# Logits of a spectral mixer made ahead of its last stage, and each batch routed in one piece

## The chip, the cores and the metric

The kernel runs on one core of a Trainium2 chip. The metric is the device time of one execution in microseconds; of several executions the median is given. TensorE (PE) multiplies matrices, its weight loads are shown as PEld; VectorE (DVE), ScalarE (ACT) and GpSimd (POOL) do the rest, and SyncE (SP) issues most DMAs.

## The reference

Two blocks follow each other: a global filter by Fourier transform along the tokens, and a mixture of experts of which each token uses the one with the largest logit. All is float32: 8 batches of 2496 tokens with 256 features, 8 experts with 1024 hidden units.

```python
X = np.fft.rfft(x, axis=1)
Y = X * (filt_r + 1j * filt_i)[None, :, :]
y = np.fft.irfft(Y, n=x.shape[1], axis=1).reshape(B * S, D)
logits = y @ w_gate
expert_idx = np.argmax(logits, axis=1)
gate_w = softmax(logits)[np.arange(N), expert_idx]
for e in range(E):
    rows = expert_idx == e
    out[rows] = gate_w[rows, None] * (np.maximum(y[rows] @ w1[e], 0) @ w2[e])
```

## The kernel before

**The transform.** 2496 = 39 x 64, so the transform of a batch is a two-dimensional one over 39 values of q and 64 values of t, in four stages of matmuls. Stage a (L348) transforms over q, three values of t at a time, and stores its result in DRAM (`zd`). Stage b (L362) reads it turned and transforms over t; VectorE multiplies the result by the filter (L369 to L378). Stage c (L388) transforms back over t: for two frequencies f at a time, it leaves in one bank of PSUM 128 rows (real and imaginary parts of 64 values of t) by 2 x 256 features. The bank is evicted and stored as u in DRAM (`ud`). Stage d (L407) reads u with 120 rows, 40 frequency parts for each of three values of t, and its matmul with the table `tds` gives y: 117 tokens (three t, 39 q) in each of 22 columns of a batch. Batch 0 keeps z and u on the chip, transposed, with features on the rows, and turns them by TensorE (`first_a`, `turn_z`, `first_c`, `turn_u`).

**Logits and routing.** After stage d, `turn_y` transposes y by TensorE (L482, 44 transposes a batch), VectorE or ScalarE evicts `yt`, and `logits` (L496) multiplies by the gate matrix `wg`, padded to 32 columns, so that four matmuls for four column strips share a bank `lt`. `turn_logits` (L507) turns the result back to tokens by experts. `route` works on at most 8 columns, so three times a batch: VectorE finds each token's expert (L529 to L543), TensorE counts the tokens of each expert ahead of each token with a triangular matrix and a matrix of ones (L554, L555), VectorE turns the counts into row numbers (L562 to L577). GpSimd then writes a token number and a gate beside each row of y and scatters the rows to DRAM in the order of experts (L615), one DMA for each column. Six tiles of y (`YB`) wait for that.

**Experts.** `tile_map` lists tiles of 128 to 512 rows of one expert. For each tile SP loads its rows (`xg`, `ng`) and the expert's weights (`w1t`, `w2t`), VectorE transposes the rows in blocks of 32x32 (L748), TensorE forms the hidden layer (L791, in a scheme with sums of quarters, or L832) and the result (L849), and GpSimd scatters the rows of the result to the output (L855).

**Order.** The order on TensorE, VectorE, ScalarE and SP is that in which the program emits instructions. Each engine works through its own in that order and waits where an operand isn't there. A planner at build time makes the order: `slot(k)` lists steps of batch k+1 (stage a), k (b and c) and k-1 (d and what follows), each with a place within the slot, the load that it needs and a cost; the main loop keeps a modelled clock `now`, emits the next step or, by a share, a step of the experts, and asks `sides` (routes, tile maps) for a few instructions after each. Stores are emitted one step after they are ordered (`move`, `flush`), loads of the next z, u and x as buffers come free (`more_loads`), weights and rows of tiles by `prefetch`. `evac` gives an eviction to VectorE or ScalarE, whichever the model has free first. PSUM has seven banks for all stages and one, `lt`, for the logits.

Of the kernel before, what the change touches and what calls it, by code (L numbers as in the profile page):

```python
# [19 lines left out]
P = 128  # L20
# [100 lines left out]
def kernel(  # L121
# [44 lines left out]

    perm = ctx.enter_context(tc.tile_pool(name="perm", bufs=1))
# [25 lines left out]
    wg = cst.tile([P, DH, CT], F32, name="wg")  # L193
# [3 lines left out]
    WM = 8  # L197

    seg = cst.tile([P, E, WM + 1], F32, name="seg")
    tot = cst.tile([P, E, WM + 1], F32, name="tot")  # L200
# [7 lines left out]
    tau_i = pro.tile([1, 64], I32, name="tau_i", bufs=1)  # L208
    pools = {}
# [31 lines left out]
    HP = P // 2  # L241
    CH = [(i0, min(4, NG - i0)) for i0 in range(0, NG, 4)]
# [23 lines left out]
    def load_rest():  # L266
        nc.sync.dma_start(out=tds, in_=td)
        nc.vector.memset(wg, 0.0)
        nc.sync.dma_start(out=wg[:, :, :E], in_=moe_w_gate.rearrange("(i p) e -> p i e", p=P))
        nc.sync.dma_start(out=ids0, in_=ids)  # L270
        nc.sync.dma_start(out=vld, in_=valid)

    def make_constants():
# [7 lines left out]
        nc.gpsimd.memset(tot, 0.0)  # L281
        nc.gpsimd.iota(prow, pattern=[[0, 1]], base=0, channel_multiplier=1)
# [18 lines left out]
    ins, outs, lgs, yts, lands = {}, {}, {}, {}, {}  # L301
    NIN, YB = 7, 6
# [78 lines left out]
    def stage_c(b, f):  # L381
# [7 lines left out]
        evac(uo[:, j:j + 2, :], p.rearrange("p (i d) -> p i d", i=2), 512)  # L389
        if j == 2:  # L390
            f0 = f - 2
            move(ud[b][:, f0:f0 + 4, :], uo[:HP])
            move(ud[b][:, NF + f0:NF + f0 + 4, :], uo[HP:])
# [3 lines left out]
    def stage_d(b, c):  # L397
        if c == 0:
            lgs[b] = sb.tile([TP, NG, E], F32, tag="lg", name="lg")
# [76 lines left out]
    def turn_y(b, c):  # L476
        yo = outs["o", b, c]
        for j in range(0, CH[c][1], 2):
            pt = bank().rearrange("p (i q) -> p i q", i=4)
            for i in range(2):  # L480
                for dh in range(DH):
                    nc.tensor.transpose(  # L482
                        pt[:, 2 * i + dh, :TP], yo[:, j + i, dh * P:(dh + 1) * P], ident[:TP, :TP]
                    )
            yt = yts[b, c, j] = sb.tile([P, 4, TP], F32, tag="yt", name="yt", bufs=4)
            evac(yt, pt[:, :, :TP], 4 * TP)

    def logits(b, g):

        js = range(min(4, NG // 2 - 4 * g))  # L490
        w = len(js) * CT
        pair = [yts.pop((b, 2 * g + j // 2, 2 * (j % 2))).rearrange("p (i h) q -> p i h q", i=2) for j in js]
        lt = psr.tile([P, 2, E * NG], F32, tag="lt", name="lt")[:, :, :TP]
        for dh in range(DH):
            for j in js:
                mm(lt[j * CT:(j + 1) * CT], lhsT=wg[:, dh, :], rhs=pair[j][:, :, dh, :],  # L496
                   start=(dh == 0), stop=(dh == DH - 1))
        ls = sb.tile([P, 2, TP], F32, tag="ls", name="ls", bufs=1)
        evac(ls[:w], lt[:w], 2 * TP)
        outs["l", b] = (g, w, ls)  # L500

    def turn_logits(b):
        g, w, ls = outs.pop(("l", b))
        n = w // CT
        pt = bank()[:TP, :2 * w].rearrange("p (i w) -> p i w", i=2)
        for i in range(2):
            nc.tensor.transpose(pt[:, i, :], ls[:w, i, :], ident[:w, :w])  # L507
        evac(lgs[b][:, 8 * g:8 * g + 2 * n, :].rearrange("p (j i) e -> p i j e", i=2),
             pt.rearrange("p i (j c) -> p i j c", c=CT)[:, :, :, :E], 16 * n)

    scatters, rows_at, held_y = {}, {}, [0]


    def route(b, c0, c1):

        t0 = 4 * c0
        w = min(4 * c1, NG) - t0
        lg = lgs[b][:, t0:t0 + w]
# [3 lines left out]
        def small(name, *shape, dt=F32, tag=None):  # L522
            n = int(np.prod(shape))
            full = sb.tile([TP, WM * n // w], dt, tag=tag or name, name=name, bufs=1)[:, :n]
            return full.rearrange("p (a b) -> p a b", a=shape[0]) if len(shape) == 2 else full

        yos = [outs.pop(("o", b, c)) for c in range(c0, c1)]
# [5 lines left out]
        yield 2  # L533
        nc.vector.tensor_tensor(ex, lg, mx[:, :, None].to_broadcast(sh3), op=ALU.subtract)
        nc.vector.tensor_tensor(oh, oh, em8[:TP, None, :].to_broadcast(sh3), op=ALU.mult)
        yield 2
        idx = small("idx", w)
        nc.vector.tensor_reduce(idx, oh, axis=AX.X, op=ALU.min)
        if t0 + w == NG:

            nc.vector.tensor_tensor(idx, idx, vld[:, t0:t0 + w], op=ALU.mult)
# [4 lines left out]
        yield 3  # L546
# [13 lines left out]
        free["s"] = max(free["s"], now[0]) + 1.2  # L560
        sd = small("sd", w)
# [3 lines left out]
        yield 3  # L565
# [4 lines left out]
        yield 2  # L570
        nc.vector.tensor_tensor(pos, pos, oe, op=ALU.mult)
        row = sb.tile([TP, WM], U32, tag="row", name="row", bufs=2)[:, :w]
        rowf = small("rowf", w)
        nc.vector.tensor_reduce(rowf, pos.rearrange("p e t -> p t e"), axis=AX.X, op=ALU.add)
        yield 2
        nc.vector.tensor_copy(row, rowf)
        nc.vector.tensor_copy(cnt, tot[:, :, w])  # L577
        yield 2
        for i, yo in enumerate(yos):
            n = min(4, w - 4 * i)  # L580
            sh8 = (TP, n, 8)
            nc.gpsimd.tensor_scalar(
                yo.bitcast(I32)[:, :n, D:D + 8], in0=ids0[:, t0 + 4 * i:t0 + 4 * i + n, None].to_broadcast(sh8),
                scalar1=float(b * S), scalar2=None, op0=ALU.add,
            )
            nc.gpsimd.tensor_copy(yo[:, :n, D + 8:], sd[:, 4 * i:4 * i + n, None].to_broadcast(sh8))
# [569 lines left out]
```

## Time and profile before

| what | value |
|---|---|
| median of 6 executions | 1564.94 us (1553.47 to 1566.86) |
| the profiled execution, its own time | 1565.88 us |
| its span, first to last instruction | 1564.2 us |
| mean granted TensorE clock | 0.980 |
| DMA packets, megabytes, mean rate | 215173, 276.82 MB, 177 GB/s |
| share of 16 DMA engines of SP's queue | 54.1% |
| SP waiting to reload `w1t` (L742) for TensorE (L791) | 232.1 us, 54 times, longest 11.7 |
| SP waiting to reload `w2t` (L738) for TensorE (L849) | 101.3 us, 30 times, longest 9.5 |

The busy time of an engine is the time in which it works on at least one instruction; matmuls overlap, so the time of a sequence is read from the starts of its members rather than from the duration of one. A granted clock of 0.5 means that TensorE runs at half speed. "Idle before" a group is the time in which the engine had nothing to do before an instruction of that group, with the engine, the tile and the line that ended it.

### The profile page before, as it was taken

Reading aid. Unit: us, or ns where it says so; the run is one execution under the profiler, and the core shown is the slowest. Engines: PE = TensorE matmul, PEld = TensorE weight load, DVE = VectorE, ACT = ScalarE, POOL = GpSimd, SP = SyncE. Lnnn points to the kernel's source line nnn. Section 1 sums busy time; section 2 is a strip of 40 time slices with the busy share of each in tenths; the row PEclk is TensorE's granted clock in tenths of the full one; section 3 lists DMA queues with packets and bytes.
Section 4 is the critical chain, followed back from the end, with each engine's and each line's share of the span. In section 5 each row is a group of like instructions: output and inputs, shape, how many; then the busy total and the mean of one; then the engine's idle time right before and its main releaser. Section 6 shows DMA issues by size and latency. Waiting matters only on the chain. (4 is left out here: it accounts for less than half of the span.)

```text
span 1564.2 us, 23882 instructions
## 1 busy us (share of the span) xinstructions
PE 1487.0 (95%) x7202; PEld 1169.3 (75%) x7202; DVE 751.7 (48%) x1676; ACT 478.7 (31%) x993; POOL 696.3 (45%) x910
## 2 busy tenths in 40 slices
PE   7988897899999999999999999999999999999998
PEld 6543454776667876787777876778888889999997
DVE  4677375415664556555674545447343534440000
ACT  3444342233232233222332223222222222223433
POOL 3343244423624555345635545665455546741111
PEclk9999899999999999999999999999999999999999
DMA  9759898887597548835494455455656443455661
GB/s 235 198 162 306 240 274 231 247 209 240 169 248 182 161 144 229 213 109 166 124 231 113 126 145 150 118 151 151 177 155 197 142 142 114 119 186 168 173 193 40
DMA packets 215173, 276.82 MB, mean 177 GB/s; under 512 B 124227, under 2 KB 162508, under 8 KB 215045
## 3 DMA queue, kind: packets, MB, share of 16 engines
q1 hardware_dynamic: 195925, 231.94, 54.1%
q0 software_dynamic: 19120, 43.33, 8.1%
q8 instruction: 61, 1.00, 0.3%
q14 instruction: 67, 0.55, 0.1%
HBM read 195.19 MB, written 80.64 MB: 176 GB/s over the span
## 5 line engine op out<-in xcount | busy, mean ns | idle before, releaser
L795 DVE TENSOR_TENSOR hT<-bank,hT 128x512 f32<-128x512 f32 (+1 forms) x504 | 300.4, 628 | 327.3 <-PE bank L791 203.6
L849 PE MATMUL bank<-w2t,hT 128*128 128x256 f32 x1984 | 446.7, 383 | 5.2 <-ACT hT L799 3.5
L849 PEld LDWEIGHTS bank<-w2t,hT 128*128 128x128 f32 x1984 | 379.0, 192 | 72.8 <-issue 15.7
L855 POOL DMA_INDIRECT out_dram<-ys,ng x161 | 161.6, 1004 | 471.3 <-DMA out_dram<-ys,ng 113.9
L799 ACT ACTIVATE hT<-hT 128x1024 f32<-128x1024 f32 (+1 forms) x144 | 132.4, 956 | 328.7 <-DVE hT L795 315.5
L615 POOL DMA_INDIRECT rows<-yo,row x176 | 177.3, 1008 | 74.9 <-issue 54.5
L791 PE MATMUL bank<-xT,w1t 128*128 128x256 f32 (+1 forms) x864 | 193.9, 361 | 1.5 <-DVE yw L371 0.9
L854 ACT ACTIVATE ys<-bank,ng 128x256 f32<-128x256 f32 x137 | 64.8, 473 | 405.4 <-PE bank L849 308.9
L791 PEld LDWEIGHTS bank<-xT,w1t 128*128 128x128 f32 x864 | 152.9, 192 | 27.4 <-issue 6.8
L791 PE MATMUL bank<-sums,wsum 128*128 128x256 f32 (+1 forms) x576 | 137.1, 361 | 0.5 <-DVE hT L795 0.4
L849 PE MATMUL bank<-w2s,hT 128*128 x592 | 132.6, 379 | 0.0
L832 PE MATMUL bank<-xT,w1t 128*128 128x128 f32 (+1 forms) x864 | 125.9, 301 | 1.8 <-DVE xT L748 1.8
L748 DVE STREAM_TRANSPOSE xT<-xg 128x512 f32<-128x512 f32 (+2 forms) x126 | 57.5, 495 | 145.7 <-PE bank L832 99.7
L832 PEld LDWEIGHTS bank<-xT,w1t 128*128 128x128 f32 x864 | 115.1, 193 | 13.0 <-issue 7.5
L849 PEld LDWEIGHTS bank<-w2s,hT 128*128 128x128 f32 x592 | 110.3, 190 | 13.8
L791 PEld LDWEIGHTS bank<-sums,wsum 128*128 128x128 f32 x576 | 101.7, 192 | 22.0 <-issue 9.4
L369 DVE TENSOR_TENSOR ys<-bank,ht 128x512 f32<-128x512 f32 x80 | 54.9, 687 | 78.2 <-PE bank L362 68.0
L348 PE MATMUL bank<-fin,tas 117*120 117x512 f32 x154 | 77.6, 624 | 6.3 <-DMA fin<-in_x_dram 5.5
L388 PE MATMUL bank<-ys,tcs 128*128 128x512 f32 x140 | 74.0, 612 | 9.9 <-DVE ys L378 6.7
L766 POOL TENSOR_TENSOR wsum<-w1t 128x256 f32<-128x256 f32 x72 | 52.7, 732 | 65.1 <-PE bank L791 63.3
L838 ACT ACTIVATE hT<-bank 128x128 f32<-128x128 f32 (+1 forms) x206 | 61.2, 298 | 51.3 <-PE bank L832 37.6
L362 PE MATMUL bank<-fin,tbs 128*128 128x512 f32 x140 | 72.0, 602 | 2.6 <-DMA fin<-zd 2.0
(143 smaller groups left out, 1626.0 us busy)
## 6 DMA issues: line engine op xcount, KB each, us to landing
w1t<-in_moe_w_dram SPq DMA_DIRECT2D x126, 512.0 KB
w2t<-in_moe_w_dram SPq DMA_DIRECT2D x68, 512.0 KB
fin<-in_x_dram SPq DMA_DIRECT2D x39, 512.0 KB
fin<-zd SPq DMA_DIRECT2D x70, 256.0 KB
ud<-uo SPq DMA_DIRECT2D x70, 256.0 KB
zd<-zo SPq DMA_DIRECT2D x35, 480.0 KB
fin<-ud SPq DMA_DIRECT2D x35, 480.0 KB
xg<-rows SPq DMA_DIRECT2D x112, 128.0 KB
```

Source lines behind the costliest of these rows:

```text
L348: mm(p[:TK, :], lhsT=tas, rhs=xt[:TP, j:j + 2, :], start=True, stop=True)
L362: mm(p, lhsT=tbs, rhs=zi[:, j:j + 2, :], start=True, stop=True)
L388: mm(p, lhsT=tcs, rhs=ys, start=True, stop=True)
L615: sc = nc.gpsimd.indirect_dma_start(out=rowsd, out_offset=bass.IndirectOffsetOnAxis(ap=at, axis=0), in_=what, in_offset=None,)
L791: mm(q[:, v], lhsT=left[:, v * P:(v + 1) * P], rhs=right, start=True, stop=True)
L795: nc.vector.tensor_tensor(o, q, a, op=ALU.add)
L799: nc.scalar.activation(o.rearrange("p v r c -> p v (r c)"), q.rearrange("p v r c -> p v (r c)"), AF.Relu)
L832: mm(p[:, :m], lhsT=w1t[2 * i + g][:, dh, fh, v * P:(v + 1) * P], rhs=xts[i][:, dh, :m], start=(dh == 0), stop=(dh == DH - 1))
L838: lambda: nc.scalar.activation(hT, p[:, :m], AF.Relu))
L849: mm(p[:, :D], lhsT=hs[i][k % 4 // 2][:, k // 4, k % 2, j * P:(j + 1) * P], rhs=w2, start=(k == 0), stop=(k == FT - 1))
L854: lambda: nc.scalar.activation(ys, p[:, :D], AF.Copy, scale=gate))
L855: nc.gpsimd.indirect_dma_start(out=out, out_offset=bass.IndirectOffsetOnAxis(ap=gis[i].bitcast(U32)[:, j, :1], axis=0), in_=ys, in_offset= ...
```

## The change

The logits are linear in y, and y is linear in u over the frequency parts: y = tds^T u for each feature. The changed kernel multiplies u by the gate matrix first and applies `tds` to the eight resulting columns.

For batches 1 to 7, VectorE transposes each bank of stage c in blocks of 32x32 into a tile `tu` of 12 or 8 frequencies, beside the eviction. `u_logits` multiplies these blocks by a gate matrix `wb` that is laid out so that the four blocks of 32 rows (two halves of t, real and imaginary part) get column groups of their own, in 64 matmuls for a batch. One matmul turns each half's result (`turn_logits`), four DMAs for each half store it in DRAM (`vd`, in elements of 32 bytes), and six DMAs load it as `spec`, 120 frequency parts by 22 columns by 8 experts (`load_logits`, emitted five modelled microseconds later). For batch 0 the transposed u is on the chip and is multiplied directly. `logits` is then one matmul with `tds` for a whole batch, and `route` runs once a batch over 22 columns, ahead of stage d. `send_rows` writes numbers and gates and scatters the rows of four columns as soon as stage d has made them; `YB` falls from 6 to 4. `turn_y` and its tiles go.

```diff
@@ stage_c
+        f0, n = HALVES[f >= HALVES[0][1]]
+        if f == f0:
+            outs["t", b] = sb.tile([P, HALVES[0][1], D], F32, tag="tu", name="tu", bufs=1)
+        nc.vector.transpose(outs["t", b][:, f - f0:f - f0 + 2, :].rearrange("p i d -> p (i d)"), p)
+        free["v"] = max(free["v"], now[0]) + 0.7
...
-    def turn_y(b, c):
...
+    def u_logits(b, half=0):
...
+        n = HALVES[half][1] // 4
+        lt = psr.tile([P, HALVES[0][1] // 4, CT], F32, tag="lt", name="lt")[:, :n]
+        tu = outs.pop(("t", b))[:, :4 * n].rearrange("p (g k) d -> p g k d", g=4)
+        for j in range(NJ):
+            for g in range(4):
+                mm(lt[g * CT:(g + 1) * CT], lhsT=wb[:, j, :], rhs=tu[:, g, :, j * CT:(j + 1) * CT],
+                   start=(j == 0), stop=(j == NJ - 1))
+        ls = outs["l", b] = sb.tile([P, HALVES[0][1] // 4 * CT], F32, tag="ls", name="ls", bufs=1)[:, :n * CT]
+        evac(ls, lt.rearrange("p k r -> p (k r)"), n * CT)
...
+    def turn_logits(b, half=0):
...
+        nc.tensor.transpose(pt, ls, ident)
+        evac(vt, pt, P)
+        for m in range(4):
+            move(vd[b][m, f0:f0 + n].rearrange("(g k) r e -> (k r) g e", g=4),
+                 vt.rearrange("p (g m e) -> p m g e", g=4, m=4)[:, m])
+        if half:
+            delayed.append((now[0] + 5.0, lambda: load_logits(b)))
+
+    def load_logits(b):
+        for th in range(2):
+            of = vd[b][2 * th:2 * th + 2].rearrange("c f r e -> (c f) r e")
+            for j in range(NB):
+                i0 = -((j - th * HT) // NB) if th else 0
+                t0 = NB * i0 + j - th * HT
+                n = (HT - 1 - t0) // NB + 1
+                nc.sync.dma_start(
+                    out=spec[b % 2][j * NS:(j + 1) * NS, i0:i0 + n],
+                    in_=of[:, t0:t0 + NB * (n - 1) + 1:NB, :],
+                )
+        lands["v", b] = now[0] + 7.0
+
+    def logits(b):
+        lgs[b] = sb.tile([TP, NG, E], F32, tag="lg", name="lg", bufs=1)
+        p = bank()[:TP, :NG * E]
+        mm(p, lhsT=tds, rhs=spec[b % 2].rearrange("p i e -> p (i e)"), start=True, stop=True)
+        evac(lgs[b].rearrange("p i e -> p (i e)"), p, NG * E)
+        sides.append(route(b))
...
+    def send_rows(b, c):
+
+        while b not in routed:
+            yield "wait"
+        row, sd, at = routed[b]
...
@@ slot
+            for half, (f0, n) in enumerate(HALVES):
+                at = (f0 + n + 4) / (NF + 4) + 0.005
+                steps.append((at, lambda half=half: u_logits(k, half), None, 2.6 if half == 0 else 2.1, "b"))
+                steps.append((at + 0.04, lambda half=half: turn_logits(k, half), None, 0.2, "b"))
...
+                    steps.append((at - 0.04, lambda: logits(k - 1), ("v", k - 1), 0.3, "d"))
...
-                if c >= 3 and c % 2:
-                    steps.append((at + 0.01, lambda c=c: logits(k - 1, (c - 3) // 2), None, 0.9, "d"))
-                if 1 <= c <= nch:
-                    steps.append((at + 0.03, lambda c=c: turn_y(k - 1, c - 1), None, 0.22 * CH[c - 1][1], "d"))
-                if c >= 3 and c % 2:
-                    later = at + (0.07 if k == 1 else 0.11)
-                    steps.append((later, lambda c=c: turn_logits(k - 1), None, 0.25, "d"))
-                    steps.append((later + 0.001, lambda c=c: sides.append(route(k - 1, c - 3, min(c - 1, nch))), None, 0.0, "d"))
+                    steps.append((at + 0.02, lambda c=c: sides.append(send_rows(k - 1, c)), None, 0.0, "d"))
```

## The prediction

> **What bounds the kernel now.** First the page's busy shares and its 40 slices:
>
> ```profile
> PE 1487.0 (95%) x7202; PEld 1169.3 (75%) x7202; DVE 751.7 (48%) x1676; ACT 478.7 (31%) x993; POOL 696.3 (45%) x910
> ...
> PE   7988897899999999999999999999999999999998
> ...
> DVE  4677375415664556555674545447343534440000
> ```
>
> TensorE sets the end: 77 us of the 1564.2 us span are idle. VectorE comes near to binding only in the third and fourth slice, 100 to 140 us. Next the groups of TensorE by shape, for the steps that the change touches (count, busy us, mean ns of one, then idle time before them):
>
> ```profile
> L482 PE MATMUL bank<-ident,yo 117*128 117x117 f32 x352 | 44.8, 269 | 2.2 <-DVE yo L234 2.2
> L496 PE MATMUL lt<-yt,wg 128*32 128x234 f32 x352 | 30.2, 379 | 9.7 <-ACT yt L234 6.7 <-DVE yt L234 2.6 <-issue 0.2
> L507 PE MATMUL bank<-ident,ls 128*117 128x128 f32 x32 | 6.2, 276 | 0.0
> L507 PE MATMUL bank<-ident,ls 96*117 96x96 f32 x16 | 3.2, 283 | 0.5 <-ACT ls L234 0.5
> L554 PE MATMUL bank<-oe,tri 117*117 117x64 f32 x32 | 5.8, 266 | 4.3 <-DVE oe L543 4.3
> L554 PE MATMUL bank<-oe,tri 117*117 117x48 f32 x16 | 3.3, 293 | 9.7 <-DVE oe L543 9.6
> ```
>
> TensorE stood idle 26.4 us before these: 9.7 before the logits (L496), 14.0 before the routing sums (L554). The duration of one is its latency; the price of one in a row is read from starts in the timeline, here at full clock (start, us, count last):
>
> ```profile
> 226.47 1.01 PE L496 MATMUL lt<-yt,wg 128*32 128x234 f32 x16
> 227.41 1.02 PE L482 MATMUL bank<-ident,yo 117*128 117x117 f32 x8
> 228.27 1.03 PE L362 MATMUL bank<-fin,tbs 128*128 128x512 f32 x2
> ```
>
> Sixteen logits instructions take 227.41 - 226.47 = 0.94 us, so four, one for each strip of 32 columns, run side by side in 0.235 us; eight transposes take 0.86 us, 0.107 each. Last the windows of 20 us (PE, PEld, DVE, ACT and POOL busy, granted clock, DMA share, GB/s):
>
> ```profile
> 100.00:120.00 20.00, 15.01 (x45) 5.89 (x44) 16.83 (x36) 6.58 (x17) 8.60 (x11) 0.90 0.69 200
> 120.00:140.00 20.00, 16.68 (x39) 7.03 (x38) 14.93 (x30) 6.21 (x14) 1.97 (x2) 0.93 0.87 287
> ...
> 180.00:200.00 20.00, 15.67 (x53) 8.20 (x53) 9.26 (x25) 6.02 (x17) 5.01 (x9) 0.83 0.81 217
> ...
> 400.00:420.00 20.00, 17.50 (x71) 12.03 (x70) 12.79 (x30) 4.07 (x10) 9.99 (x16) 0.83 0.30 87
> ...
> 1100.00:1120.00 20.00, 20.00 (x94) 17.61 (x93) 10.81 (x17) 5.54 (x7) 10.90 (x16) 1.00 0.58 174
> ```
>
> A gap costs twice: after one of some 2 us the clock is halved for a while. The 3.8 us gap before L496 at 187 us stands in a window granted 0.83, the 2.3 us gap before L554 at 410 us in another. Nine windows with a gap of L482, L496 or L554 above 2 us (at 180, 400, 420, 440, 580, 900, 940, 1000 and 1020 us) were granted 0.83, 0.83, 0.92, 0.91, 0.93, 0.91, 0.91, 0.92 and 0.94: together 0.90 of a window is lacking, 18 us. After 1040 us there is expert work alone, unbroken, and nothing of this change.
>
> **TensorE work.** Removed: 352 transposes of y x 0.107 = 37.7; 88 rounds of logits x 0.235 = 20.7; 48 turns of logits (L507) x 0.11 = 5.3; 24 routing pairs x 0.48 (two passes of L554 and two of L555, 237.41 to 237.89 us in the same timeline) = 11.5. Together 75.2 us. Added, by the instruction order of the changed kernel: 448 small matmuls of 96 or 64 columns, each in two passes, four strips at once, 224 rounds. No row has such a round. From below, 234-column rounds scaled by columns give 112 x 0.096 + 112 x 0.064 = 18; from above, 224 x 0.235 = 53. I take 0.11 us, the start-to-start of a 64-column pass that has to load its weights (L555): 24.6. Eight one-matmul logits (176 columns, two passes, between L555's 0.11 and a 256-column pass's 0.215; by columns 0.148): 2.4. Eight routing pairs of 176 columns: 32 x 0.148 = 4.7. Fourteen turns x 0.11 = 1.5. Batch 0 from the transposed u: four rounds at 0.43 (a 512-column pass), four at 0.235, four passes and six turns at 0.11: 3.7. Together 36.9. **Net -38**, with bounds -45 and -10. Around 100 to 140 us TensorE waits for VectorE anyway, so one batch's share, 38/8 = 5, is not realised: **-33**.
>
> **VectorE.** 70 transposes of a 128x512 bank are added. L748 takes 686 ns from SBUF, a copy of a bank of that size 684 to 690 ns: 0.69 each, 48 us. The 28 evictions of yt and ls (17.2 us) go. Sixteen small operations of a route cost 93 us over 24 routes; eight wide ones, at some 0.37 us each (0.25 us for 64 elements, plus 112 more at the slope 0.69/512 to 0.42/256 = 1.05 ns), cost 8 x 16 x 0.37 = 47. Net -15: nothing is added in busy time. Where TensorE waits for these transposes is priced below.
>
> **Waits removed.** 26.4 us of gaps and 18 us of clock: **-44**.
>
> **Waits added.** (1) The way through DRAM. After the second turn of a batch, eviction 0.4 us, four stores at 0.4 us of SP issue and 2.9 us to the last packet (as the 64-byte loads of ng, 2 to 3 us after issue), six loads at 0.44 and again 2.9: 10.4 us, if SP is free. In the new order TensorE has between that turn and the logits that need it 14.6, 8.6, 15.5, 20.7, 17.3, 15.6 and 7.8 us of work for batches 1 to 7 (counts x starts as above). SP is seldom free: it waited 54 times, 232 us, to reload w1t (4.3 us each) and the stores and loads are queued behind such reloads, behind the gathers of xg and ng, and ahead of the next z, u and weight loads, which come later by as much. With one such wait the way takes 14.7: TensorE idles 6.1 in batch 2 and 6.9 in batch 7, 13 us, and 3 of clock: 16. With none: 4.4. With two (19 us): 34 and some 13 of clock. (2) The routing sums, L554's successors. The seven VectorE steps ahead of them grow from 7 x 0.25 to 7 x 0.37, 0.9 us more. TensorE's cover between logits and sums is 4.3, 4.3, 13.7, 3.4, 4.3, 7.8, 6.9 and 5.2 us; before, by the same count, ten of 24 had under 4.4, and six gaps of 0.4 to 3.3 make up the 14 us. So four gaps of 2 + 0.9 and one of 1: 12.6, and 4 x 2 of clock (18 us over nine gaps): 21; bounds 0 and 8 x 5.3 = 42. (3) Logits that wait for the last VectorE transpose, and turns that wait for the eviction just ahead. In batches 1 to 3 the second half's last three matmuls of stage three are followed at once by the logits: VectorE then has four products (2.8 us) and three transposes (2.1) to do in TensorE's 2.6: 2.3 us each; four turns stand right behind their logits, 0.8 us each; three drops of clock: 15 in all; bounds 0 and 45. A wait of TensorE here holds the expert matmuls behind it; ScalarE and VectorE then run dry, but catch up. **Together +52**, bounds 4 and some 125.
>
> The 98 new DMAs are 0.4 us x 98 = 39 us of SP, whose 377 us of issues leave room, and 5120 packets of 32 bytes a batch. The trace's 64-byte packets take 13.6 ns: 5120 x 13.6 / 16 = 4.4 us of all engines for each batch; the queue's mean packet (54.1% x 16 x 1564 / 195925 = 69 ns) gives 22. Both lie beside other work, except that they lengthen (1).
> The Trainium skill, "DMA: Bandwidth & Descriptors", section "Specifications", speaks against this: it says that a transfer under 512 bytes makes the DMA engine read, modify and write. That would put the 32-byte stores nearer to the 69 ns than to the 13.6 ns, which only 64-byte reads show; the sum above goes by 13.6, and by the other the stores alone would take (69 - 13.6) x 2560 / 16 = 9 us longer for each batch, which would make the forecast the slower rival below. No row here has a 32-byte store to DRAM.
>
> **Sum.** 1565.9 - 33 - 44 + 52 = **1541 us**; its base, the profiled execution, is 0.9 us above the median of 1564.9, so 1540.
>
> **Rivals.**
> A: the new waits are covered. The expert work between the steps speaks for it, the covers of 8 us against it. 1566 - 38 - 44 + 20 = 1504.
> B: the early stretch swallows the gain. VectorE binds until expert work comes in; DMA share is 0.7 to 1.05 up to 400 us. If the work taken off TensorE in three of eight batches only becomes idle time (15) and the waits are 70: 1566 - 23 - 44 + 70 = 1569, no change. For it: gaps before L388 are VectorE's. Against: most routing gaps lie later.
> C, slower: the way through DRAM. If stores sit behind two or three weight reloads and small packets take the mean's time, the way takes 25 us. Then each batch waits at its logits: 10.4, 16.4, 9.5, 4.3, 7.7, 9.4 and 17.2, 75 us, and 7 x 3.4 of clock, 99 in the place of 16: 1624. It decides from a way of some 19.5 us, where (1) reaches 50 and the sum 1575.
>
> **Chances.** Forecast 0.42, A 0.22, B 0.17, C 0.19. The forecast's own range is 1515 to 1565. Faster by over 0.5% (under 1557), which is about what this measurement can tell: most of the forecast and A, 0.62. Within 0.5%: 0.16. Slower: C and a part of B, 0.22. The range for 8 in 10 leaves out the far half of A and of C: 1505 to 1585.
>
> **What would show it.** TensorE's busy time falls by 35 to 40 us; rounds of new logits start some 0.11 us apart; gaps before the one-matmul logits in batches 2 and 7 of 5 to 8 us; gaps of 2 to 3 us before the routing sums; the mean clock stays near 0.98; from 1040 us on, nothing changes but its start. I am wrong if the small rounds cost 0.2 us, if logits wait in most batches, or if these waits are not there at all.

## The result, and the profile after

The changed kernel takes 1553.29 us (median of 22 executions, 1543.35 to 1562.72) against 1560.99 us for the kernel before on the same chips (48 executions, 1553.23 to 1568.45): a ratio of 0.9947, with a 95% interval of 0.9932 to 0.9962. By the ratio that is a gain of 8.3 us (7.7 between the two medians), where 25 us were forecast. The profiled execution of the changed kernel took 1550.8 us (span 1549.1), 2.5 below its median; that of the kernel before lies 4.9 above its own. So the two traces differ by 15.1 us, of which some 7 are the scatter of single executions.

First the page of the changed kernel, its busy shares and its slices:

```profile
PE 1446.4 (93%) x7354; PEld 1139.6 (74%) x7354; DVE 739.2 (48%) x1479; ACT 444.5 (29%) x870; POOL 699.9 (45%) x911
...
PE   7977886889999999899989999799999999999998
...
DVE  4665565245575556556558355246443434440000
```

TensorE is busy 40.6 us less than before, and yet its share of the span falls from 95 to 93%: a good part of what it no longer does has become idle time. Of the 40 slices, five from the third to the ninth, some 80 to 350 us, have lost a tenth, and a 7 has come in at the twenty-sixth, between 968 and 1007 us. Next the groups of TensorE that answer to those shown of before (count, busy us, mean ns of one, then idle time before them and what ended it):

```profile
L525 PE MATMUL lt<-tu,wb 128*32 128x96 f32 x448 | 16.5, 269 | 9.9 <-issue 7.4 <-DVE tu L406 2.5
L525 PE MATMUL lt<-tu,wb 128*32 128x64 f32 x448 | 11.7, 234 | 4.1 <-issue 2.1 <-DVE av L700 1.1 <-DVE tu L406 0.8
L551 PE MATMUL bank<-ident,ls 128*64 128x128 f32 x7 | 2.3, 322 | 2.9 <-ACT ls L238 2.9
L575 PE MATMUL bank<-spec,tds 120*117 120x176 f32 x16 | 5.8, 453 | 30.6 <-DMA spec<-vd 25.7 <-DMA fin<-ud 4.9
L618 PE MATMUL bank<-oe,tri 117*117 117x176 f32 x16 | 3.7, 312 | 0.0
```

The 26.4 us that TensorE stood idle for logits and routing are gone: the routing sums (L618, before L554) no longer wait at all. In their place stand 30.6 us before the one-matmul logits (L575), which wait for `spec`, the logits that come back from DRAM (4.9 of it, in batch 2, the list puts down to `fin`, but there too the logits start 1.7 us after the last load of `spec` is issued), and 16.9 us before the small matmuls (L525) and their turns (L551). The windows show the price in clock (busy us of PE, PEld, DVE, ACT, POOL, then granted clock, DMA share, GB/s):

```profile
180.00:200.00 20.00, 15.22 (x94) 9.04 (x93) 5.06 (x8) 2.33 (x7) 8.14 (x12) 0.74 0.53 164
400.00:420.00 20.00, 20.00 (x134) 13.76 (x133) 12.02 (x18) 6.97 (x15) 13.78 (x18) 1.00 0.90 287
620.00:640.00 20.00, 13.63 (x54) 10.91 (x53) 11.71 (x25) 4.80 (x11) 6.61 (x9) 0.83 0.86 187
960.00:980.00 20.00, 7.77 (x27) 5.35 (x26) 5.77 (x14) 3.30 (x5) 4.32 (x7) 0.73 0.90 180
1100.00:1120.00 20.00, 20.00 (x94) 17.60 (x94) 6.74 (x11) 4.64 (x7) 11.41 (x15) 1.00 0.62 173
```

The window at 180 us, granted 0.83 before, has 0.74: a slow burst of small matmuls stands in it, of which more at the end. The window at 400 us, granted 0.83 before, is now full at 1.00. Those at 620 and 960 us hold the waits of batches 5 and 7, with the clock at 0.83 and 0.73. The one at 1100 us is as before: expert work alone.

What ends the wait of batch 7 is read from SP's own queue, the timeline of its DMA issues (start us, us of issue, what is moved, count):

```profile
956.44 1.61 SPq L804 DMA_DIRECT2D w2t<-in_moe_w_dram  x2
958.15 6.07 SPq L320 DMA_DIRECT2D vd<-vt  x4
965.45 1.97 SPq L775 DMA_DIRECT2D xg<-rows  x4
967.61 0.40 SPq L779 DMA_DIRECT2D ng<-rows  x1
968.88 2.26 SPq L775 DMA_DIRECT2D xg<-rows  x4
971.34 0.40 SPq L779 DMA_DIRECT2D ng<-rows  x1
971.78 3.38 SPq L566 DMA_DIRECT2D spec<-vd  x6
```

and from TensorE's timeline at the same time, where the bracket is the idle time before the line:

```profile
956.50 0.27 PE L551 MATMUL bank<-ident,ls 128*64 128x128 f32 x1
...
962.65 1.89 PE L857 MATMUL bank<-xT,w1t 128*128 128x256 f32 x8
976.77 0.91 PE L575 MATMUL bank<-spec,tds 120*117 120x176 f32 x2 [12.23 <-DMA spec<-vd]
```

The second turn runs at 956.50 us and SP has issued the stores (`vd`) by 964.2. Then SP gathers the rows of two expert tiles (`xg`, `ng`), and only at 971.8 come the six loads of `spec`. The logits start 1.6 us after the last of them is issued. TensorE had 8.0 us of work meanwhile, close to the 7.8 that the prediction counted, and stands for 12.2.

The same count for batches 1 to 7, from the second turn to the one-matmul logits, gives 24.6, 15.3, 15.9, 21.6, 24.0, 24.6 and 20.3 us, a mean of 20.9. In parts: 3.1 us to the first store's issue, 3.2 for issuing four stores, 8.6 from the last store to the first load, 4.3 for issuing six loads, 1.7 to the logits. The largest part is the one between the stores and the loads. The idle time before the logits is 2.3, 4.9, 0.1, 0.6, 6.4, 4.2 and 12.2 us for these batches: five wait for more than 2 us, where the sum had waits in batches 2 and 7 alone.

The span can be laid out in three parts that add up to it: TensorE's work at full clock (its busy time less half of what lay in stretches granted half the clock), what that half clock cost, and idle time.

| kernel | span | work at full clock | lost to half clock | idle | of it before L575 |
|---|---|---|---|---|---|
| before | 1564.2 | 1460.6 | 26.4 | 77.2 | – |
| after | 1549.1 | 1414.3 | 32.1 | 102.7 | 30.6 |

The change takes 46.3 us of work off TensorE and gives back 25.5 in idle time and 5.7 in clock.

### The profile page after: what moved, and what is told of

It reads as the page before. It is cut to its first block, busy times and chain, and to the rows that moved or that the text cites. A ratio compares the mean times of both kernels' runs of the same rounds, so it can differ in the third digit from the quotient of the medians.

```text
span 1549.1 us, 23874 instructions
## 1 busy us (share of the span) xinstructions
PE 1446.4 (93%) x7354; PEld 1139.6 (74%) x7354; DVE 739.2 (48%) x1479; ACT 444.5 (29%) x870; POOL 699.9 (45%) x911
## 5 line engine op out<-in xcount | busy, mean ns | idle before, releaser
L915 PE MATMUL bank<-w2t,hT 128*128 128x256 f32 x1984 | 443.9, 381 | 0.2 <-ACT hT L870 0.2
L915 PEld LDWEIGHTS bank<-w2t,hT 128*128 128x128 f32 x1984 | 378.5, 191 | 70.0 <-issue 16.3
L857 PE MATMUL bank<-xT,w1t 128*128 128x256 f32 (+1 forms) x864 | 190.2, 356 | 0.4 <-DVE hT L861 0.4
L857 PEld LDWEIGHTS bank<-xT,w1t 128*128 128x128 f32 x864 | 152.2, 190 | 26.0 <-issue 7.0
L898 PEld LDWEIGHTS bank<-xT,w1t 128*128 128x128 f32 x864 | 118.1, 196 | 25.9 <-issue 15.1
L898 PE MATMUL bank<-xT,w1t 128*128 128x128 f32 (+1 forms) x864 | 129.7, 306 | 7.9 <-issue 4.6
L857 PE MATMUL bank<-sums,wsum 128*128 128x256 f32 (+1 forms) x576 | 135.2, 357 | 1.0 <-DVE yw L384 0.5
L915 PE MATMUL bank<-w2s,hT 128*128 x592 | 132.6, 379 | 0.0
L915 PEld LDWEIGHTS bank<-w2s,hT 128*128 128x128 f32 x592 | 110.3, 190 | 13.8
L857 PEld LDWEIGHTS bank<-sums,wsum 128*128 128x128 f32 x576 | 101.3, 190 | 24.3 <-issue 10.0
L361 PE MATMUL bank<-fin,tas 117*120 117x512 f32 x154 | 76.2, 615 | 13.2 <-DMA fin<-in_x_dram 13.2
L406 DVE STREAM_TRANSPOSE tu<-bank 128x512 f32<-128x512 f32 x70 | 49.4, 709 | 73.9 <-ACT uo L238 65.6
```

Source lines behind the costliest of these rows:

```text
L361: mm(p[:TK, :], lhsT=tas, rhs=xt[:TP, j:j + 2, :], start=True, stop=True)
L857: mm(q[:, v], lhsT=left[:, v * P:(v + 1) * P], rhs=right, start=True, stop=True)
L898: mm(p[:, :m], lhsT=w1t[2 * i + g][:, dh, fh, v * P:(v + 1) * P], rhs=xts[i][:, dh, :m], start=(dh == 0), stop=(dh == DH - 1))
L915: mm(p[:, :D], lhsT=hs[i][k % 4 // 2][:, k // 4, k % 2, j * P:(j + 1) * P], rhs=w2, start=(k == 0), stop=(k == FT - 1))
```

## The experiments

Each was timed in five rounds beside the kernel before on the same chip. The ratios below are to that kernel. The theory on trial (R in the expectations) is that the way through DRAM, held up in SP's queue, takes what the forecast expected to gain.

**The changed kernel once more (e1_control).** No edit.

> The changed kernel once more, beside the other runs of this chip: 0.993 to 0.997 of the time of the kernel before. Every theory expects this.

Measured: 1549.53 us, 0.9953 [0.9926, 0.998]; 33.2 us idle before L575, 11.7 before L525, 107.4 in all, work 1415.7. The second trace tells what the first told, and their idle times agree within 5 us. It is of the slowest of twelve executions (1555.7 of 1539.0 to 1555.7), so what follows is judged by the ratios; traces tell where the time lies.

**The wait taken away (e2_stale).** Each batch is routed by the logits of the batch before, so this kernel leaves out the right routing, and with it the wait.

```diff
-        mm(p, lhsT=tds, rhs=spec[b % 2].rearrange(...), start=True, stop=True)
+        mm(p, lhsT=tds, rhs=spec[max(b - 1, 0) % 2].rearrange(...), start=True, stop=True)
```

> Batches 1 to 7 are routed by the logits of the batch before, which have long landed, so the one matmul (L575) waits for no DMA; all stores, loads and instructions stay, and the order on TensorE, VectorE, ScalarE and SP too. Tokens go to experts of other tokens' choice, as many as before. Theory R (the way through DRAM gives the gain back): the 30.6 us of idle time before L575 go, and with them some 10 us of halved clock: 30 to 40 us less than the changed kernel, 0.970 to 0.976 of before. Theory T (VectorE's transposes, which wait for ScalarE's eviction of the same bank, hold the rest): the wait moves to the next instruction, less than 10 us are gained, above 0.988.

Measured: 1536.51 us, 0.9896 [0.986, 0.9933]; idle before L575 0.0. The idle time falls from the control's 107.4 to 86.8, which is less than the 33.2 that went, although this trace is of the fastest of its six executions. The group of e2_stale that took a part of it:

```profile
L857 PE MATMUL bank<-sums,wsum 128*128 128x256 f32 x448 | 116.8, 383 | 15.5 <-POOL wsum L833 14.5 <-POOL sums L821 0.7 <-DVE yw L384 0.3
L575 PE MATMUL bank<-spec,tds 120*117 120x176 f32 x16 | 3.8, 319 | 0.0
```

It is one gap of 14.5 us at 990 us. GpSimd's timeline shows why: routed earlier, batch 7 puts its row scatters ahead of `wsum`, the sums of the weights for the next expert tile.

```profile
950.64 1.08 POOL L681 DMA_INDIRECT rows<-yo,row  x1 [1.92 <-DVE hT L861]
952.03 0.99 POOL L681 DMA_INDIRECT rows<-yo,row  x1 [0.30 <-issue]
...
966.88 1.02 POOL L921 DMA_INDIRECT out_dram<-ys,ng  x1 [0.16 <-issue]
968.21 1.00 POOL L681 DMA_INDIRECT rows<-yo,row  x1 [0.30 <-issue]
...
988.02 0.99 POOL L681 DMA_INDIRECT rows<-yo,row  x1 [0.30 <-issue]
...
989.84 0.72 POOL L833 TENSOR_TENSOR wsum<-wsum,w1t 128x256 f32<-128x256 f32 x1
```

In a row, a scatter comes every 1.3 us, and the `wsum` that TensorE needs at 990.61 us is ready only after the last of them. The order on TensorE, VectorE, ScalarE and SP is that of the control; GpSimd's is not, so the gap is a mixture of the missing wait and another order there. What follows: without the wait the kernel is some 0.6% faster (the two intervals, 0.986 to 0.9933 and 0.9926 to 0.998, just overlap), about 9 us where theory R expected 30 to 40, and not the whole of the missing 17 us. How much the other order on GpSimd takes back isn't shown apart.

**VectorE's transpose ahead of the eviction (e3_turnfirst).** VectorE's waits in the changed kernel list 65.6 us in which `tu` (L406) waits for ScalarE's eviction of the same bank (L238), up to 11.5 us at a time (us in all, times, longest):

```profile
DVE tu L406 <- ACT uo L238: 65.6, 19, 11.5
```

The rival theory (T) was that this holds back the small matmuls and makes the second turn, and so the stores, late.

```diff
-        evac(uo[:, j:j + 2, :], p.rearrange("p (i d) -> p i d", i=2), 512)
         ...
         nc.vector.transpose(outs["t", b][...], p)
+        evac(uo[:, j:j + 2, :], p.rearrange("p (i d) -> p i d", i=2), 512)
```

> VectorE's transpose of a bank is emitted ahead of the eviction of the same bank, so that it waits for TensorE alone and the eviction waits for it. Theory T: VectorE's 65.6 us of waiting for ScalarE go, the gaps inside and before the small matmuls (some 14 us) shrink: 10 to 20 us less than the changed kernel. Theory R: within 4 us of it.

Measured: 1553.01 us, 0.9998 [0.9976, 1.0021]; 34.8 us idle before L575, 12.2 before L525. No gain. VectorE's wait for ScalarE is gone, and in its place ScalarE's evictions `uo` wait 112.2 us for VectorE's transposes; yet the small matmuls, which need the transposes, wait as long as in the control (12.2 against 11.7 us). So VectorE's waiting is not what holds them. The stores came no earlier (4.3 us from the turn to the first issue, against 3.1), so whether a second turn that was free of both engines would help is not shown.

**Loads right behind the stores (e4_behind).** The six loads enter SP's queue directly after the four stores instead of five modelled microseconds later.

```diff
-            delayed.append((now[0] + 5.0, lambda: load_logits(b)))
+            moves[1].append(lambda: load_logits(b))
```

> The six loads are emitted straight behind the second half's four stores, instead of five modelled microseconds later, so ahead of the gathers of rows that stand between them. SP then waits some 3 us for the stores to land. Theory R: the way from the turn to the logits falls from 15 to 25 us to 10 to 15 us, the idle time before L575 from 30.6 to under 15, and the time by 10 to 25 us. Theory T: within 4 us.

Measured: 1554.87 us, 1.0005 [0.9979, 1.003]. The edit does what it should: from last store to first load 4.4 us instead of 8.6, the wait before the logits nearly halved. With nothing left between them, these 4.4 us are the time until the stores have landed, so about half of the 8.6 was that, and the other half what SP did in between. Yet nothing is gained; GpSimd's sums are late in its place (groups of e4_behind):

```profile
L857 PE MATMUL bank<-sums,wsum 128*128 128x256 f32 x448 | 120.2, 392 | 19.1 <-POOL wsum L833 12.5 <-POOL sums L821 6.2 <-DVE yw L384 0.3
L575 PE MATMUL bank<-spec,tds 120*117 120x176 f32 x16 | 5.2, 414 | 17.9 <-DMA spec<-vd 17.9
```

The control has 6.2 us before all of L857. The longest of these waits, 8.7 us at 1015 us, is again one for a `wsum` that stands behind GpSimd's row scatters.

**Half of the small matmuls (e5_half).** The logits of batches 1 to 7 leave out half of the features.

```diff
-        for j in range(NJ):
+        for j in range(NJ // 2):
         ...
-                   start=(j == 0), stop=(j == NJ - 1))
+                   start=(j == 0), stop=(j == NJ // 2 - 1))
```

> The small matmuls of batches 1 to 7 take four of the eight blocks of features only: the logits are made of half the features, 32 instructions in two passes for each batch and half are left out in a burst of 64. At full speed a whole burst takes 1.46 or 1.03 us, so 7 x 1.25 = 8.7 us of work go. Theory B (TensorE is short of instructions in these bursts, which take 31 us in batches 1 to 3 in the place of 7.5): the stalls inside them shrink by half or more, and 15 to 25 us are gained on the changed kernel. Theory R: 8 us, hardly more, and the idle time before L575 stays near 31 to 33 us.

Measured: 1541.77 us, 0.9913 [0.9889, 0.9937], some 6 us below the changed kernel by the ratios, whose intervals just overlap: near theory R's 8 rather than the 15 to 25 of theory B. Work falls by 13.8 us against the control, and the fourteen bursts of small matmuls take 24.8 us instead of 43.0, from the first to the next instruction's start. That is 18 us for half of them, about twice what their full speed would cost: from batch 4 on a burst of 64 takes 1.46 us (96 columns) or 1.03 us (64 columns), seventeen for all fourteen. The wait before L575 is no smaller, 37.7 us. So in the control the bursts take 43 us from first to last, idle time and halved clock within them included, where 24.6 and a part of 15 were priced; 30.3 of it is in batches 1 to 3.

**Needed later (e6_later).** The planner is told that the loads land ten microseconds later, and places the logits accordingly.

```diff
-        lands["v", b] = now[0] + 7.0
+        lands["v", b] = now[0] + 17.0
```

> The planner takes the loaded logits to land 17 modelled microseconds after the issue of the loads, not 7, and puts the one matmul that needs them, and stage d behind it, later by so much. Theory R: idle time before L575 falls from 31 to 33 us to under 8, and the time by 15 to 30 us, if the later rows find no one waiting. If the wait only moves to the next in line (y rows, gathers): within 5 us of the changed kernel.

Measured: 1546.22 us, 0.995 [0.9932, 0.9968], no gain on the changed kernel. Most of the wait goes, and others come (groups of e6_later):

```profile
L915 PE MATMUL bank<-w2t,hT 128*128 128x256 f32 x1984 | 444.8, 382 | 13.4 <-DMA w2t<-in_moe_w_dram 12.8 <-ACT hT L870 0.6
L525 PE MATMUL lt<-tu,wb 128*32 128x96 f32 x448 | 19.2, 295 | 11.4 <-issue 7.0 <-DVE tu L406 4.3
L575 PE MATMUL bank<-spec,tds 120*117 120x176 f32 x16 | 4.0, 331 | 5.3 <-DMA spec<-vd 3.3 <-DMA fin<-ud 2.0
```

In the changed kernel L915 waits 0.2 us. With the logits put off, the expert work that fills the time waits for weights (`w2t`) that have not landed.

**One tile of y less in the kernel before (e7_before_yb5).** The change cuts `YB` from 6 to 4, which the prediction did not price. The kernel before was run with five.

```diff
-    YB = 6
+    YB = 5
```

> The kernel before with five tiles of y in the place of six. If fewer tiles of y cost much of what the change gains (ScalarE's evictions of y wait for the scatter of an earlier tile, 6 us at 90 us of the changed kernel): 1.003 to 1.010 of before. If the way through DRAM is the cause: 0.998 to 1.002.

Measured: 1567.07 us, 1.0079 [1.0052, 1.0107], with 20.2 us idle before stage c (L388) where the kernel before has 9.9. In that kernel a tile of y is worth 12 us by the medians; the two traces don't show them, since that of the kernel before is of an execution above its median and both spans are 1564 us. This doesn't carry over as it stands, since the changed kernel scatters y earlier. What may be its share there is one gap of 5.8 us at 93 us (L485), just after ScalarE has stood 2.4 us before an eviction of y; that it waits there for a free tile is inferred. The changed kernel with six tiles was not run, so this rival stays open.

**Both moves together (e8_behind12).** Loads behind the stores, and the logits five modelled microseconds later.

```diff
-            delayed.append((now[0] + 5.0, lambda: load_logits(b)))
+            moves[1].append(lambda: load_logits(b))
         ...
-        lands["v", b] = now[0] + 7.0
+        lands["v", b] = now[0] + 12.0
```

> The loads straight behind the stores, and the landing taken as 12 modelled microseconds after them: the loads come 5 to 10 us sooner and the matmul that needs them about when it does now. Theory R: idle time before L575 under 8 us in the place of 31 to 33, 15 to 30 us gained on the changed kernel, unless GpSimd's order, which is made by the builder and not by hand, gives a new stall, as it did in the two kernels before with 12 to 19 us.

Measured: 1544.08 us, 0.993 [0.9905, 0.9955]; 7.6 us before L575, 12.0 before the sums of L857, idle 97.0, clock 28.5. Better than the loads moved alone, by 0.7%: its idle time is 97.0 us against 106.0. Theory R expected 15 to 30 us, and against the changed kernel (0.9947 and 0.9953) hardly 0.2% is left. What 12.0 alone does was not run.

**Another queue (e9_actq).** ScalarE issues the stores, as soon as it has evicted the turn, and the loads. TensorE's order is that of the changed kernel.

```diff
-            move(vd[b][m, f0:f0 + n].rearrange(...), vt.rearrange(...)[:, m])
+            nc.scalar.dma_start(out=vd[b][m, f0:f0 + n].rearrange(...), in_=vt.rearrange(...)[:, m])
         ...
-                nc.sync.dma_start(
+                nc.scalar.dma_start(
                     out=spec[b % 2][j * NS:(j + 1) * NS, i0:i0 + n],
```

> Stores and loads of the logits are issued by ScalarE instead of SP; the order of everything else is that of the changed kernel. Theory R: with no gathers and reloads ahead of them, the way from the turn to the matmul that needs them falls from 15 to 25 us to 10 to 15, the idle time before L575 from 31 to 33 us to under 15, and SP comes sooner to x, rows and weights: 10 to 25 us gained on the changed kernel. Against it: ScalarE waits some 2 us for the stores to land and spends 0.4 us on each of 98 issues, which holds back its evictions; if that decides, no gain or a loss.

Measured: **1531.13 us, 0.9836 [0.9803, 0.9869]**, the best of all, 24 us below the kernel before on the same chip, and 1.1% below the changed kernel by the two ratios, whose intervals are far apart. The order on TensorE and VectorE is that of the changed kernel; GpSimd's is not. Batch 7 in the timeline of ScalarE of e9_actq:

```profile
938.73 0.25 ACT L238 COPY vt<-bank 64x128 f32<-64x128 f32 x1
939.01 2.73 ACTq L554 DMA_DIRECT2D vd<-vt  x4
946.12 4.53 ACTq L566 DMA_DIRECT2D spec<-vd  x6
950.69 0.59 ACT L870 COPY hT<-bank 128x512 f32<-128x512 f32 x1 [11.71 <-DMA spec<-vd]
```

The first store is issued 0.8 us after the turn, and the last load is out 12.5 us after it, against 18.7. Over the seven batches the mean to the last load's issue is 10.8 us, against 19.2. The groups of e9_actq:

```profile
L857 PE MATMUL bank<-xT,w1t 128*128 128x256 f32 x672 | 166.1, 384 | 6.9 <-ACT hT L870 6.9
L857 PE MATMUL bank<-sums,wsum 128*128 128x256 f32 x448 | 116.7, 383 | 7.3 <-POOL wsum L833 7.0 <-DVE yw L384 0.3
L575 PE MATMUL bank<-spec,tds 120*117 120x176 f32 x16 | 4.7, 379 | 6.0 <-DMA spec<-vd 5.5 <-DMA xg<-rows 0.6
```

The wait before the logits is 6.0 us. ScalarE pays a little: its eviction at 950.69 stands behind the loads, and TensorE waits 6.9 us for it. The trace (work 1412.8, clock 29.4, idle 92.7) is of an execution near the slowest of its six, 1536.6 of 1524.2 to 1537.3, and shows less of the gain than the median.

**Another queue, and the logits later (e10_actq12).** The edit of e9_actq with 12.0 for 7.0 in `lands`.

```diff
-        lands["v", b] = now[0] + 7.0
+        lands["v", b] = now[0] + 12.0
```

> The same, and the landing taken as 12 modelled microseconds: idle time before L575 under 4 us; 3 to 10 us less than with 7.

Measured: 1539.8 us, 0.9913 [0.9879, 0.9946]; 1.9 us before L575, idle 92.4, clock 28.5. The wait is smaller still, the time larger. The two intervals are apart, so it is slower than e9_actq, though both have the whole way on ScalarE's queue. The sums of the two traces are within 3 us of each other, but the idle time lies elsewhere (9.7 us before L375, 0.0 in e9_actq), and the orders on TensorE differ. Why it is slower stays open.

**Stores alone on ScalarE (e11_actst).** The first half of the edit of e9_actq on top of e8_behind12; the loads stay with SP.

```diff
-            move(vd[b][m, f0:f0 + n].rearrange(...), vt.rearrange(...)[:, m])
+            nc.scalar.dma_start(out=vd[b][m, f0:f0 + n].rearrange(...), in_=vt.rearrange(...)[:, m])
```

> The stores by ScalarE, the loads by SP one step behind the turn, landing taken as 12: idle time before L575 under 8 us, as with both on SP straight behind each other; the time within 5 us of that kernel (0.993 of before). If ScalarE's issues cost much, worse than it.

Measured: 1541.8 us, 0.9908 [0.988, 0.9937]; 7.9 us before L575. Against e8_behind12, where SP issues both, 0.9908 to 0.993: the intervals overlap, so the stores by themselves are not shown to be worth anything.

**Loads alone on ScalarE (e12_actld).** Only the second half of the edit of e9_actq.

```diff
-                nc.sync.dma_start(
+                nc.scalar.dma_start(
                     out=spec[b % 2][j * NS:(j + 1) * NS, i0:i0 + n],
```

> The changed kernel with only the six loads of the logits (spec, L566) issued by ScalarE; the stores (vd, L320) stay on SP's queue. It parts the two halves of what e9_actq moved. Theory Q (what costs the time is that the loads stand in SP's queue behind gathers and weight loads: in the changed kernel 8.6 us on the mean from the last store's end of issue to the first load's issue, against 2.3 us from the turn to the first store's issue): nearly all of e9's gain comes with the loads alone. Then the wait before the one-matmul logits falls from 31 to 33 us to at most 12, and the ratio to the kernel before lies at 0.982 to 0.989. Rival S (the stores are what counts: they go out late, and a load of the logits, wherever it is issued, waits for their landing): the wait stays above 20 us and the ratio at 0.992 to 0.998, as for the changed kernel itself. Rival E (ScalarE now stands still at its loads until the stores have landed, and its evictions are late): waits of matmuls on ScalarE's work grow by over 8 us and the ratio is 0.993 or above with the wait before the logits gone.

Measured: 1545.78 us, 0.9932 [0.991, 0.9955], with 6.3 us before L575. Of the expectation's three, Q asked for a ratio of 0.982 to 0.989 and fails, S for a wait above 20 us and fails; rival E fits: the wait is mostly gone and the time isn't. In ScalarE's waits of e12_actld stand

```profile
ACT uo L238 <- DMA spec<-vd: 22.8, 2, 17.0
ACT hT L865 <- DMA spec<-vd: 17.7, 2, 10.3
ACT hT L870 <- DMA spec<-vd: 13.6, 1, 13.6
```

(us in all, times, longest), 54 us in these three. The longest is batch 1, where the stores wait 9 us in SP's queue and ScalarE stands with them (timelines of ScalarE, VectorE and TensorE):

```profile
139.97 7.13 ACTq L566 DMA_DIRECT2D spec<-vd  x6
147.15 0.59 ACT L238 COPY uo<-bank 128x512 f32<-128x512 f32 x1 [17.02 <-DMA spec<-vd]
```

```profile
147.77 0.72 DVE L406 STREAM_TRANSPOSE tu<-bank 128x512 f32<-128x512 f32 x1 [11.02 <-ACT uo L238]
...
150.50 0.77 DVE L814 STREAM_TRANSPOSE xT<-xg 128x256 f32<-128x256 f32 x2
```

```profile
151.04 2.47 PE L898 MATMUL bank<-xT,w1t 128*128 128x256 f32 x5 [13.37 <-issue]
```

VectorE waits for ScalarE's eviction, and TensorE for the `xT` that VectorE makes after it. So with the loads alone moved, TensorE pays elsewhere what it no longer waits at the logits. e9_actq, with both halves moved, gains 0.96% more and the intervals are apart; but e10_actq12 has both halves there too, and its 0.9913 does not differ from e12_actld's 0.9932 beyond the intervals. That both halves must move fits e9_actq, but is not shown. The trace of e12_actld is again of an extreme execution, the fastest of six (1536.7 of 1536.7 to 1550.0).

## Why the prediction was partly right

Set out in the same parts, for the profiled execution, the prediction's sum and what the traces show:

| term, us | predicted | measured |
|---|---|---|
| TensorE work | -33 | -46.3 |
| old waits, idle | -26.4 | -26.4 |
| (1) way through DRAM, idle | +13 | +30.6 |
| (2) routing sums, idle | +12.6 | 0.0 |
| (3) small matmuls and turns, idle | +10.1 | +16.9 |
| idle elsewhere | 0 | +4.4 |
| clock, old and new together | -2 | +5.7 |
| sum | -25.7 | -15.1 |

The way through DRAM is idle time before L575. The predicted idle of (3) is 3 x 2.3 and 4 x 0.8; the predicted clock is the 18 us won less the 3, 8 and 4.9 that (1), (2) and (3) were charged.

**The step that failed** is (1) of the waits added: "With one such wait the way takes 14.7: TensorE idles 6.1 in batch 2 and 6.9 in batch 7, 13 us". Measured are 30.6 us, 12.2 of them in batch 7 and 12.9 in batches 1, 5 and 6, which the sum had free of waits. That logits wait in most batches was one of its signs of being wrong. The way takes 20.9 us on the mean (21.3 in the control). The work counted as cover was not the fault, since it was right or counted too short: in e2_stale, where the logits wait for nothing, TensorE takes 22.0, 10.5, 15.7, 20.8, 17.4, 20.4 and 7.9 us from turn to logits, beside the 14.6, 8.6, 15.5, 20.7, 17.3, 15.6 and 7.8 that were counted (in batches 1 and 6 some other waits lie in between). What was mis-sized is SP's part. The sum had 0.4 us to the first store, 1.6 for its four issues, 2.9 to its landing, 2.6 for six loads and 2.9 to theirs, 10.4 with SP free, and a single wait of 4.3 us for a reload of `w1t`. Measured are 3.1, 3.2, 8.6, 4.3 and 1.7. Of the 8.6 some 4.4 remain in e4_behind, where nothing stands between; the rest is SP's other work, in batch 7 the gathering of rows for two expert tiles. Such work sits there in the queue because `load_logits` is emitted five modelled microseconds after the stores, and prefetches of experts come in between. The row for it was at hand: the gathers stand in the list of DMA issues. Rival C named the mechanism and gave it 99 us, with a way of 25; the measured way of 21 lies between the two, a little above the point of 19.5 from which C was to decide. Even so the kernel didn't become slower, since (2) and the TensorE work came out better than priced, by 12.6 and 13.3 us, while (1), (3), the clock and idle time elsewhere came out worse by 17.6, 6.8, 7.7 and 4.4. That the time still lies within the forecast's 1515 to 1565 us is luck: errors of both signs cancelled. In the stated bounds for all waits, those of the three terms (47, 42 and 45) make 134 us rather than 125, which changes nothing else.

**TensorE work.** Right in kind, 13 us more than priced. With each matmul's time read from its start to the next one's, at full clock and without idle time, the steps removed took 78.5 us (75.2 priced) and the steps added 36.2 (36.9 priced), the small matmuls 23.3 of it (24.6 priced). The steps that the change leaves alone came out 4.0 us shorter, and the 5 us set aside as "not realised" around 100 to 140 us belong to idle time in this layout. A burst that runs through is faster than priced, with rounds of 0.091 and 0.064 us (1.46/16 and 1.03/16) where 0.11 was taken: there the lower bound, scaled by columns, was right.

**(2) Routing sums.** Wrong: 0.0 us. In the changed kernel VectorE is done with `oe` 2.9 to 4.0 us after the logits of a batch (7.4 in batch 2), where the sum's upper bound had up to 5.3, and TensorE comes to the sums 3.6 to 9.6 us after them (28.6 in batch 2): each time VectorE is ahead. In e8_behind12 and e11_actst, where the logits come at another place, 4.0 and 4.4 us appear at L618, in the other variants 1.3 at most.

**(3) Small matmuls.** The gaps are 16.9 us instead of 10.1, but they are not the ones that were described. Only 3.3 us wait for VectorE's transposes, 2.9 for the eviction ahead of the turn; 9.5 are put to nothing ("issue"). The 14.0 before L525 all lie within bursts, none ahead of their first matmul.

**Unpriced.** Perhaps the tiles of y (5.8 us at L485); and an x load that lands late, which makes 10.7 us of the idle time before L361 at 249 us, where the kernel before stands 4.8 us at its own (L348, 255 us). Every variant of the changed kernel waits for 8 to 15 us there, e9_actq 14.1: no experiment was made on it.

**VectorE, DMA.** Its busy time fell by 12.5 us, forecast 15. The Trainium skill, "DMA: Bandwidth & Descriptors", section "Specifications", has DMA engines read, modify and write for transfers under 512 bytes. Whether they do here no run shows. The prediction's 9 us a batch rest on another premise, that a 32-byte element takes the 69 ns of a mean packet, and that isn't seen. In e9_actq these stores and loads have a queue to themselves:

```profile
q10 hardware_dynamic: 37156, 1.15, 1.3%
```

that is 1.3% of 16 engines' span of 1534.9 us, over 37156 packets: some 8.6 ns each. Loads alone, in e12_actld, are 18340 packets with 0.7%, some 9.4 ns. At that, the 5120 packets of a batch take 16 engines some 3 us, against a way of 20.9: most of its length is not theirs.

What the runs settle: the wait before the logits follows what stands in SP's queue. It is 30.6 to 33.2 us with the changed kernel's order, 17.9 with the loads straight behind the stores (e4_behind), 6.0 with stores and loads on another queue (e9_actq). What they don't settle is what that wait costs in time. With none (e2_stale) the kernel is some 0.6% faster. In e6_later, e8_behind12, e10_actq12, e11_actst and e12_actld the wait is 1.9 to 7.9 us and the ratios are 0.995, 0.993, 0.9913, 0.9908 and 0.9932, against the changed kernel a gain of less than 0.5%. Only e9_actq reaches the forecast's size, 1.6% below the kernel before, and more than e2_stale has without any wait, so its gain isn't the wait alone. In the changed kernel and its variants with the full computation idle time stays between 92 and 107 us, and a wait taken from one place comes up in GpSimd's sums, in weight loads or in ScalarE's evictions. Which order would keep the gain, and why e9_actq does better than the others, stays open.

## What to carry to other kernels

Here a result that goes to DRAM and back took 20.9 us, twice the 10.4 of its bare parts: list what the queue's owner will issue from the store to the load, from the trace, before pricing it. A short urgent transfer can go on the queue of an engine that has no prefetches to issue; then look at what that engine is kept from, as ScalarE was for 17.0 us in e12_actld, where it had the loads but not the stores. When a wait is moved within an order made by a planner, look for it again elsewhere before counting the gain: here five variants out of six that cut it to under 8 us kept less than 0.5%.

## What the runs showed that was not expected

The bursts of small matmuls run at two speeds. Batch 4 of the changed kernel, then batch 3, in TensorE's timeline:

```profile
408.12 1.53 PE L525 MATMUL lt<-tu,wb 128*32 128x96 f32 x64
```

```profile
318.03 0.87 PE L525 MATMUL lt<-tu,wb 128*32 128x96 f32 x32
319.89 0.32 PE L525 MATMUL lt<-tu,wb 128*32 128x96 f32 x3 [0.99 <-issue]
320.65 0.26 PE L525 MATMUL lt<-tu,wb 128*32 128x96 f32 x1 [0.44 <-issue]
321.35 0.87 PE L525 MATMUL lt<-tu,wb 128*32 128x96 f32 x28 [0.44 <-issue]
```

The same 64 instructions take 1.46 us to the next start, and 4.1; at worst 9.05, at 180 us. The pauses, some 0.4 to 1 us each, wait for nothing that the profile shows, and in the second case the clock was full. All six bursts of batches 1 to 3 are slow, 31.5 us in all (5.6, 4.3, 9.05, 5.2, 4.1 and 3.2), and of the eight later ones only two take longer than 2 us. The other variants with 64 instructions to a burst share the pattern, 38.8 to 44.1 us for the fourteen against 44.5, but for e6_later: 51.4, with batch 3's second burst at full speed (1.03 us, at 330 us) and batch 4's first slow (6.35, at 416 us). So it doesn't hang on the batch alone. What holds TensorE back there was not tried and stays open.
